# First-batch scores as 64x64 array tiles, and the last two pieces' first FFN layer by Strassen's seven products

## The chip, the cores and the metric

One core of a Trainium2 chip runs the whole program. Its engines are PE (TensorE, matrix products; PEld is its loading of stationary operands), DVE (VectorE), ACT (ScalarE), POOL (GpSimd) and SP, which here only starts transfers (ACT starts some too). The metric is device time in microseconds of one launch, the median of the runs; lower is better.

## The reference

Block-causal attention over 8 batches x 8 heads x 576 tokens x 64 dimensions, then a two-layer FFN on its output (4608 tokens x 512, hidden width 2048):

```python
def _attn_ref(q, k, v) -> np.ndarray:
    ...
    block = 64
    scores = scale * np.matmul(q, k.transpose(0, 1, 3, 2))
    mask = block_i >= block_j          # blocks of 64 tokens
    scores = np.where(mask, scores, -1000000000.0)
    scores = scores - np.max(scores, axis=-1, keepdims=True)
    attn = np.exp(scores)
    attn = attn / (np.sum(attn, axis=-1, keepdims=True) + 1e-09)
    return np.matmul(attn, v).astype(np.float32)

def _moe_ref(x, w_in, w_out) -> np.ndarray:
    h = x @ w_in
    relu6 = np.clip(h + 3.0, 0.0, 6.0)
    g = h * relu6 / 6.0
    return (g @ w_out).astype(np.float32)
```

The two weight matrices arrive as 64-bit floats and are brought to 32 bits on the chip.

## The kernel before

**Work.** Attention runs over 32 slots (batch x pair of heads; `n` is the slot). The FFN runs over 13 pieces of the token axis, numbered 0 to 12. Most have 384 tokens; pieces 0 and 3 have 192. Piece 11 holds tokens of the last two batches, piece 12 the last 384 tokens.

**Precision.** From the second batch on, every operand is split into two 16-bit parts, hi and lo, and each product is three 16-bit products (hi·hi, hi·lo, lo·hi). `h` is the first FFN layer of a piece: for each of the 16 slices `f` of 128 hidden units, four 128-deep steps x three part products x two halves `h`, each half a 128x64 stationary operand into 64 output partitions. The two halves' matmuls run side by side in the array. `o` is the second layer (18 such matmuls of 512 columns for one `f` of a 384-token piece). Between them stand `r` (ACT activation from PSUM, then a DVE op), and `g` (hi by ACT or DVE, lo by DVE).

**First batch.** Slots 0 to 3 are computed in 32-bit while the weights load. `qk_load32` and `qk_load32_rest` bring q and k of the first three blocks (tile `qf`) and the other six (`qr`). `qk_prep32` transposes them (tile `qt`, by `ident`) and evicts `kT` and `qd`; in `qd` each block's two heads lie on the diagonal of a 128x128 operand whose other two quarters POOL zeroes. `s_block32` makes the scores `sf` of one block of 64 queries x both heads by one full-array matmul over all keys up to that block. Then come the row maximum `st` (DVE), the exponential `pf` (ACT), transposes `pt` by PE, evictions `pT`, and `pv_group32`, which spreads the row sums by one product `pr` and multiplies by v into `pf`. Piece 0 is also 32-bit.

**Weights.** `w_load` loads raw 64-bit words (tiles `rawi`, `rawo`, or parts of `x`), ACT makes `exi`/`exo` from the high words, DVE shifts the low words (`sgi`/`sgo`) and joins both. `w_max` and `w_split` scale them and make the 16-bit parts.

**Order.** Nothing is issued as it is written. The functions hand their instructions to `Recorder`, with a key (a due time from the tables `AS`, `RT`, `AT`, `FT` and others), and `schedule` plays an engine model (`cost`) and emits one fixed order for each engine. Where an operation lists several engines ("AV"), the planner picks one. Nearly every instruction therefore shows as line 489 (518 after the change), where `emit` calls the engine, and is told apart by its tile name. In the built program each transfer that SP or ACT starts uses one of eight semaphores in turn, and its start waits, in its engine's queue, until the earlier transfer on that semaphore has landed.

**Buffers.** PSUM has three `s` banks, two `h` banks and three `o` banks. The inputs of four pieces are held at a time, `xb[pc % 4]`.

## Time and profile before

| | |
|---|---|
| time, median of 3 runs (lowest to highest) | 1007.56 us (1006.49 to 1008.28) |
| the profiled execution's own time | 1008.51 us |
| its span, first to last instruction | 1006.7 us |
| PE / PEld busy | 980.4 / 724.6 us |
| DVE / ACT / POOL busy | 813.4 / 624.0 / 62.3 us |
| granted TensorE clock, mean | 0.998 |

The profile's "busy" of PE is the union of its matmuls with ends that are modelled, so a PE that is busy all the time can still be running its columns more slowly than elsewhere. The time from one instruction's start to the next one's start in the timeline tells the rate. "Idle before, releaser" names what ended a wait.

### The profile page before, as it was taken

To read this page: it belongs to the slowest core of one execution; us is meant where nothing else is said; L and a number is where in the kernel's file an instruction comes from. 1 tells how busy PE (TensorE), PEld (TensorE's weight loads), DVE (VectorE), ACT (ScalarE), POOL (GpSimd) and SP (SyncE) were. 2 spreads that over 40 slices of the span, in tenths; PEclk is the share of its full clock that TensorE was granted. 3 is DMA by queue.
4 is the path that set the end of the run, shared out by engine and by line. 5 is a ranking of instruction groups with operands and counts; after the bars stand their busy time and mean duration, and the time that the engine had idled before them with its cause. 6 is when DMAs were issued, how large, how long until landed. Compare 5 with 4: busy or idle time off the path is not lost. (4 is left out here: it accounts for less than half of the span.)

```text
span 1006.7 us, 29038 instructions
## 1 busy us (share of the span) xinstructions
PE 980.4 (97%) x11681; PEld 724.6 (72%) x11681; DVE 813.4 (81%) x2266; ACT 624.0 (62%) x1508; POOL 62.3 (6%) x237
## 2 busy tenths in 40 slices
PE   5999999999999999999999999999999999999998
PEld 4666656767777876677777776677777777777776
DVE  5899998999999999999999999888887776333332
ACT  3889866766667767676676665666666555343332
POOL 2122200000000000000000000000000000000000
PEclk9999999999999999999999999999999999999999
DMA  9694687899799977988997886766574373000000
GB/s 244 206 277 114 126 152 132 134 177 210 117 140 208 172 139 146 151 163 127 160 170 136 152 166 109 142 129 119 101 152 88 72 128 56 5 33 2 33 1 32
DMA packets 412535, 128.90 MB, mean 128 GB/s; under 512 B 399984, under 2 KB 401776, under 8 KB 412400
## 3 DMA queue, kind: packets, MB, share of 16 engines
q1 hardware_dynamic: 365408, 111.41, 58.4%
q10 hardware_dynamic: 46992, 15.64, 7.1%
q8 instruction: 91, 1.49, 0.6%
q14 instruction: 44, 0.36, 0.1%
HBM read 45.09 MB, written 9.44 MB: 54 GB/s over the span
## 5 line engine op out<-in xcount | busy, mean ns | idle before, releaser
L489 PE MATMUL h<-x,win 128*64 128x384 f16 (+2 forms) x4720 | 435.1, 320 | 1.1 <-DVE r L489 0.9
L489 PE MATMUL o<-wout,g 128*64 128x512 f16 (+3 forms) x3336 | 411.8, 379 | 0.0
L489 PEld LDWEIGHTS <-win 128*64 128x64 f16 (+1 forms) x4632 | 297.1, 110 | 70.5 <-issue 3.3
L489 PEld LDWEIGHTS <-g 128*64 128x64 f16 x3360 | 222.7, 110 | 108.2 <-issue 0.5
L489 ACT ACTIVATE r<-h,eg,sh 128x384 f32<-128x384 f32 (+1 forms) x240 | 137.3, 593 | 126.0 <-PE h L489 119.9
L489 ACT ACTIVATE p<-s,st,esc 128x64 f32<-128x64 f32 (+1 forms) x280 | 163.1, 587 | 72.2 <-DVE st L489 61.3
L489 DVE SCALAR_TENSOR_TENSOR r<-r,eg,h 128x384 f32<-128x384 f32 (+1 forms) x192 | 113.3, 591 | 103.3 <-ACT r L489 103.2
L489 DVE SCALAR_TENSOR_TENSOR phl<-p,st,phl 128x128 f16<-128x128 f32 (+4 forms) x252 | 135.7, 582 | 0.1
L489 ACT ACTIVATE g<-r 128x384 f16<-128x384 f32 (+1 forms) x149 | 75.7, 508 | 86.4 <-DVE r L489 83.9
L489 DVE SCALAR_TENSOR_TENSOR g<-r,g 128x384 f16<-128x384 f32 (+1 forms) x192 | 102.9, 536 | 31.1 <-ACT g L489 30.2
L489 DVE TENSOR_REDUCE st<-s 128x1 f32<-128x64 f32 (+1 forms) x280 | 117.9, 446 | 1.3 <-PE s L489 1.1
L489 PE MATMUL s<-qkT 128*64 128x64 f16 (+7 forms) x1120 | 95.7, 287 | 1.8 <-DVE x L489 0.8
L489 ACT ACTIVATE phl<-p,st 128x256 f16<-128x256 f32 (+4 forms) x130 | 68.2, 557 | 34.6 <-DVE st L489 18.7
L489 PEld LDWEIGHTS <-vhl 128*64 128x64 f16 x1680 | 72.1, 110 | 17.1 <-issue 9.1
L489 PE MATMUL pv<-pT,vhl 128*64 128x192 f16 (+2 forms) x1680 | 73.7, 233 | 5.2 <-ACT x L489 2.2
L489 PEld LDWEIGHTS <-qkT 128*64 128x64 f16 x1120 | 58.8, 110 | 24.8 <-issue 6.8
L489 ACT ACTIVATION_READ_ACCUMULATOR p<-s,st,esc 128x1 f32 x280 | 55.2, 197 | 0.0
L489 POOL MEMSET p<- 128x64 f32 x140 | 21.9, 156 | 528.7 <-DVE phl L489 504.7
L489 DVE TENSOR_SCALAR phl<-p,st 128x384 f16<-128x384 f32 (+4 forms) x122 | 47.0, 417 | 1.8
L489 DVE SCALAR_TENSOR_TENSOR qks<-qk,rs_q,qks 128x576 f16<-128x576 f32 x56 | 44.1, 810 | 0.1
L489 DVE TENSOR_REDUCE qkmx<-qk 128x2 f32<-128x1152 f32 x24 | 32.3, 1344 | 4.2 <-DMA qk<-in_k_dram 3.8
L489 DVE TENSOR_SCALAR st<-st,esc 128x3 f32<-128x3 f32 (+1 forms) x168 | 33.9, 210 | 0.7
(162 smaller groups left out, 781.3 us busy)
## 6 DMA issues: line engine op xcount, KB each, us to landing
out_dram<-osb SPq DMA_DIRECT2D x35, 256.0 KB, 2.3
qk<-in_k_dram SPq DMA_DIRECT2D x21, 288.0 KB, 4.7
rawo<-in_moe_w_out_dram SPq DMA_DIRECT2D x11, 512.0 KB, 4.5
qk<-in_q_dram SPq DMA_DIRECT2D x19, 288.0 KB, 3.6
vnat<-in_v_dram ACTq DMA_DIRECT2D x40, 128.0 KB, 4.7
vnat<-in_v_dram SPq DMA_DIRECT2D x24, 128.0 KB, 3.6
rawi<-in_moe_w_in_dram SPq DMA_DIRECT2D x6, 512.0 KB, 3.9
qk<-in_q_dram ACTq DMA_DIRECT2D x9, 288.0 KB, 4.8
```

The costliest lines, as they stand in the source:

```text
L489: getattr(eng, method)(*args, **kw)
```

## The change

**Score tiles.** `s_pair32` takes the place of `s_block32`. A block's two heads become two 64x64 matmuls (64-deep, 64 outputs) on two quarters of the array, and two blocks are issued as one group of four; blocks 2, 4, 5 and 8 (`SWAP`) send head 0 to output partitions 64 to 127, so that a group's four matmuls name four different quarters. `qd` and its zeroing go; `qT` is plain. Since swapped blocks have their heads on exchanged partitions, `pr` and the 32-bit `pf` of a group are made in two sets, the swapped one with the constant `cross` in place of `halves`. The scores of block 8 are cut at 512 and not at 320.

**Long runs.** q and k of the first batch are loaded with 3 or 6 consecutive tokens on a partition: runs of 768 and 1536 bytes, where they were 512 and 256. Transposes become 64x64 matmuls against `ident`, written with a stride: 144 in all, where there were 32 of 96 columns and 24 full-array transposes.

**Strassen.** For pieces 11 and 12 two slices `f` and two halves of the tokens form a 2x2 block product, made by seven products `m` of 192 columns (`h_pair`; 84 matmuls of 192 columns) in place of eight (48 of 384). `w_comb` makes the four sums of weight blocks for each of 8 chunks (`wr`, `wq`, `ws`), `x_comb` the four sums of inputs for each of the two pieces (`xr`, `xt`; the result lies in an `xb` that is free by then). Seven DVE instructions and one of ACT gather the products in `hf` and `hu`, from which `r` then reads.

**The rest.** The shift of the weights' low words may go to POOL. The planner learns of the eight outstanding transfers (`LANES`) and of run lengths, can take several tiles in one step, and gets other numbers in its tables. Both of the last pieces now wait, in the order in which they are written, for all attention of both.

The order changes on every engine. First, ACT's queue at the very start. The names: `qf`, `qr`, `vnat` and `raw`/`x` are loads of q and k, of v and of weights; `pf_0` is the first exponential. Before:

```order
L489 DMA rawi_1_107<-in_moe_w_in_dram 128x2x512
L489 DMA vnat_102<-in_v_dram 64x2x64
L489 DMA qf_180<-in_q_dram 96x2x128
L489 DMA x_82<-in_moe_w_out_dram 128x1024
L489 ACT_TABLE_LOAD
L489 ACTIVATE pf_0_120,sums_0_117<-sf_0_0_119,st_0_118 128x64
```

and now:

```order
L518 ACT_TABLE_LOAD
L518 ACTIVATE qkf_113<-qt_1_114 128x192
L518 DMA qr_168<-in_q_dram 64x384
L518 DMA qr_168<-in_k_dram 64x384
L518 DMA qf_140<-in_q_dram 64x192
L518 ACTIVATE qkf_123<-qt_0_125 128x192
L518 DMA qf_140<-in_k_dram 64x192
L518 DMA vnat_102<-in_v_dram 64x2x64
L518 DMA rawi_0_105<-in_moe_w_in_dram 128x2x512
L518 DMA qf_183<-in_q_dram 64x192
L518 DMA qf_183<-in_k_dram 64x192
L518 ACTIVATE pf_0_121,sums_0_119<-sf_0_0_118,st_0_120 128x64
```

The table load and two evictions moved ahead of the first exponential, and the load of a second weight block (`x_82`), which stood directly before it, went to SP's queue.

Second, PE in the later blocks of slot 0 (`pt` transposes of the exponentials). Before:

```order
L489 MATMUL sf_5_0_234<-qkf_112 128x384
L489 MATMUL pr_0_214<-rd_0_213,halves 128x192
L489 MATMUL pt_3_0_227<-ident,pf_3_210 128x128 x2
L489 MATMUL pt_4_0_242<-ident,pf_4_224 128x128 x3
L489 MATMUL pf_0_216<-pT_0_160,vnat_101 64x64
L489 MATMUL pt_1_0_225<-ident,pf_1_221 128x128
L489 MATMUL sf_6_0_248<-qkf_112 128x448
```

and now:

```order
L518 MATMUL pt_3_0_230<-ident,pf_3_211 128x128 x2
L518 MATMUL pt_4_0_246<-ident,pf_4_213 128x128 x2
L518 MATMUL h_0_268<-x_81,win 128x192
L518 MATMUL sf_5_0_238<-qkf_113 64x384 x2
L518 MATMUL sf_6_0_239<-qkf_113 64x448 x2
L518 MATMUL pt_1_0_228<-ident,pf_1_225 128x128
```

Blocks 5 and 6, which stood apart as full-array matmuls, now stand together as four 64x64 ones.

Third, DVE where piece 10 ends and piece 11 begins. Before (`x_81<-pv` is the last slot's attention going into piece 12):

```order
L489 SCALAR_TENSOR_TENSOR x_81<-pv_1_2273,x_81 128x192
L489 SCALAR_TENSOR_TENSOR r_14_2200<-r_14_2200,eg_724,h_14_2199 128x384
L489 SCALAR_TENSOR_TENSOR g_14_2201<-r_14_2200,g_14_2201 128x384
L489 SCALAR_TENSOR_TENSOR r_15_2204<-r_15_2204,eg_724,h_15_2203 128x384
L489 SCALAR_TENSOR_TENSOR g_15_2205<-r_15_2204,g_15_2205 128x384
L489 SCALAR_TENSOR_TENSOR r_0_2236<-r_0_2236,eg_724,h_0_2235 128x384
```

and now:

```order
L518 SCALAR_TENSOR_TENSOR r_14_2216<-r_14_2216,eg_723,h_14_2215 128x384
L518 SCALAR_TENSOR_TENSOR ws_2261<-wq_2260,ws_2261 128x8x128
L518 SCALAR_TENSOR_TENSOR g_14_2217<-r_14_2216,g_14_2217 128x384
L518 TENSOR_TENSOR wq_2263<-wr_2262 128x256 x2
L518 TENSOR_TENSOR wq_2263<-wq_2263,wr_2262 128x256
L518 TENSOR_TENSOR wq_2263<-wr_2262,wq_2263 128x256
L518 SCALAR_TENSOR_TENSOR r_15_2220<-r_15_2220,eg_723,h_15_2219 128x384
L518 TENSOR_TENSOR wr_2265<-win 128x1024
L518 SCALAR_TENSOR_TENSOR g_15_2221<-r_15_2220,g_15_2221 128x384
L518 TENSOR_TENSOR hf_0_0_2268<-m_0_2_2272,hf_0_1_2269 128x2x96
```

The weight sums stand between the `r` and `g` of piece 10's last slices, and run on into the first gathering of products.

The core of the diff:

```diff
--- before
+++ after
+SWAP = (2, 4, 5, 8)
...
-RT = (25.619, 55.46, 59.881, 70.769)
+LANES = 8
+RT = (25.6, 42.4, 59.9, 77.0)
...
-            return 600, 2000 + nb / (290 if nb >= 400000 else 210), False
+            run = min(self.run(outs[0]), self.run(args[1] if len(args) > 1 else ins[0]))
+            return 600, 2000 + nb / (205 if run <= 256 else 260 if run <= 512 else 310 if run < 1500 else 340), False
...
+                    if e != "gpsimd" and ways[e][0][0][0] == "dma_start" and len(lanes) >= LANES:
+                        r = lanes[-LANES] if lanes[-LANES] > t else None
...
-        nc.vector.tensor_scalar(sg.bitcast(U32), lw, 29, None, op0=ALU.logical_shift_right)
+        nc.add([
+            ("gpsimd", "tensor_scalar", (sg.bitcast(I32), lw, T_SCALE, -0.5), dict(op0=ALU.mult, op1=ALU.add)),
+            ("vector", "tensor_scalar", (sg.bitcast(U32), lw, 29, None), dict(op0=ALU.logical_shift_right)),
+        ][:TWAYS])
...
+        nt = NTR if rest else NTA
+        if rest:
+            t = natp.tile([P, 2, nt, D], F32, tag="qk", bufs=2, name=f"qr{n}")
+        else:
+            t = attp.tile([P, 2, nt, D], F32, tag="vhl", bufs=2, name=f"qf{n}")
+        c0, c1 = (T0, S) if rest else (0, T0)
                 nc.load(
-                    t[:, s, :, h], src[0, 2 * n + h, T0:].rearrange("(t p) d -> p t d", p=P), AQ
+                    t[h * BLK:(h + 1) * BLK, s].rearrange("p t d -> p (t d)"),
+                    src[0, 2 * n + h, c0:c1].rearrange("(p t) d -> p (t d)", t=nt), AQ,
                 )
         qn[n] = t
...
-                parts = [o[:, :S], o[:, S:3 * S]]
+                qkT[n] = o[:, :S], o[:, S:]
...
-                    nc.tensor.transpose(
-                        ps[:, u * P:(u + 1) * P], t[:, s, u].rearrange("p h d -> p (h d)"), ident
+            nt = NTR if rest else NTA
+            nc.joint = "qt", n, s, rest
+            for u in range(nt):
+                for h in range(2):
+                    hb = slice(h * BLK, (h + 1) * BLK)
+                    nc.tensor.matmul(
+                        ps[hb, u:nt * BLK:nt], t[hb, s, u], ident[hb, hb], start=True, stop=True
                     )
...
+    def s_pair32(n, *blocks):
+        kT, qT = qkT[n]
+        pss = {}
+        nc.joint = "sf", n, blocks
+        for i in blocks:
+            nk = BLK * (i + 1)
+            pss[i] = [(0, min(nk, 512), ps_s.tile([P, 512], F32, tag="s", name=f"sf{n}_{i}_0"))]
+            s_mm32(n, i, *pss[i][0], 2 * len(blocks))
+        nc.joint = None
+        for i in blocks:
+            nk = BLK * (i + 1)
+            if nk > 512:
+                pss[i].append((512, nk, ps_s.tile([P, 512], F32, tag="s", name=f"sf{n}_{i}_1")))
+                nc.joint = "sf", n, i
+                s_mm32(n, i, *pss[i][1], 2)
+                nc.joint = None
+            s_soft32(n, i, pss[i])
+    def s_mm32(n, i, c0, c1, ps, share):
+        kT, qT = qkT[n]
+        nc.share = share
+        for h in range(2):
+            r, o = h * BLK, (h ^ (i in SWAP)) * BLK
+            nc.tensor.matmul(
+                ps[o:o + BLK, :c1 - c0], qT[r:r + BLK, i * BLK:(i + 1) * BLK], kT[r:r + BLK, c0:c1],
+                start=True, stop=True,
+            )
+        nc.share = 2
+    def s_soft32(n, i, pss):
...
-        chunks = [(0, nk)] if nk <= 512 else [(0, 320), (320, nk)]
-            w = max(c1 - c0, P)
-            nc.tensor.matmul(
-                ps[:, :w], qd[:, qi].rearrange("p h x -> p (h x)"), kT[:, c0:c0 + w],
-                start=True, stop=True,
-            )
...
-        nc.tensor.matmul(pr, halves, rd.rearrange("p i x -> p (i x)"), start=True, stop=True)
+        sets = []
+        for w in range(2):
+            b = [i for i in range(GB) if (g * GB + i in SWAP) == w]
+            sets.append((w, b[0], b[-1] + 1))
+        nc.joint = "pr", n, g
+        for w, b0, b1 in sets:
+            nc.tensor.matmul(
+                pr[:, b0 * BLK:b1 * BLK], (halves, cross)[w], rd[:, b0:b1].rearrange("p i x -> p (i x)"),
+                start=True, stop=True,
+            )
...
+        for w, b0, b1 in sets:
+            js = [j for j in range(nj) if 2 * j - 3 * g < b1]
+            for j in js:
+                i0 = max(b0, 2 * j - 3 * g)
+                kp = BLK if 2 * j + 1 > 3 * g + 2 else P
+                a = i0 * NU[g] + j
+                us = slice(a, a + (b1 - 1 - i0) * NU[g] + 1, NU[g])
+                for h in range(2):
+                    o = (h ^ w) * BLK
+                    nc.tensor.matmul(
+                        ps[h * D:(h + 1) * D, i0 * BLK:b1 * BLK],
+                        vnat[n % NVB][:kp, j, h, :],
+                        t[:kp, us, o:o + BLK],
+                        start=(j == 0),
+                        stop=(j == js[-1]),
+                    )
+        nc.joint = None
         if g == 0:
...
+    def w_comb(c):
+        r = attp.tile([P, NDT, NH], F32, tag="qks", bufs=1, name=f"wr{c}")
+        plus(r, win[:, c, :, 0], win[:, c, :, 1])
+        o = attp.tile([P, 4, 2, P], F32, tag="phl1", bufs=1, name=f"wq{c}")
+        a11, a12, a21, a22 = (r[:, 2 * j:2 * j + 2, i * P:(i + 1) * P] for i in range(2) for j in range(2))
+        nc.vector.tensor_add(o[:, 0], a21, a22)
+        nc.vector.tensor_sub(o[:, 1], o[:, 0], a11)
+        nc.vector.tensor_sub(o[:, 2], a11, a21)
+        nc.vector.tensor_sub(o[:, 3], a12, o[:, 1])
+        tag = SW_TAGS[c]
+        pool = {"qk": natp, "raw": ffp}.get(tag, attp)
+        bufs = 2 if tag in ("qk", "qkT", "pT2") else 1
+        t = pool.tile([P, 4, 2, 2, P], F16, tag=tag, bufs=bufs, name=f"ws{c}")
+        hi, lo = (t.rearrange("p i j l x -> p (i j) l x")[:, :, l] for l in range(2))
+        o8 = o.rearrange("p i j x -> p (i j) x")
+        nc.scaled(hi, o8, E_S, "AV")
+        nc.vector.scalar_tensor_tensor(lo, o8, E_S, hi, op0=ALU.mult, op1=ALU.subtract)
+        sw[c] = t
...
+    def x_comb(pc):
+        x, xt = xb[pc % 4], x_terms(pc)
+        for j in range(2):
+            b = []
+            for jj in (j, j + 2):
+                t = attp.tile([P, TP], F32, tag="p", bufs=NPB, name=f"xr{pc}_{jj}")
+                plus(t, x[:, 0, jj], x[:, 1, jj])
+                b += [halves_of(t, 0), halves_of(t, 1)]
+            b11, b12, b21, b22 = b
+            ts = [attp.tile([P, 2, HT], F32, tag="p", bufs=NPB, name=f"xt{pc}_{j}_{i}") for i in range(2)]
+            t1, t2, t3, t4 = (t[:, i].rearrange("p (s k) -> p s k", s=2) for t in ts for i in range(2))
+            nc.vector.tensor_sub(t1, b12, b11)
+            nc.vector.tensor_sub(t2, b22, t1)
+            nc.vector.tensor_sub(t3, b22, b12)
+            nc.vector.tensor_sub(t4, t2, b21)
+            for i, t in enumerate(ts):
+                hi, lo = (xt[:, 2 * i:2 * i + 2, l, j] for l in range(2))
+                nc.scaled(hi, t, E_S, "AV")
+                nc.vector.scalar_tensor_tensor(lo, t, E_S, hi, op0=ALU.mult, op1=ALU.subtract)
...
+        def product(m, wsel, xsel):
+            if len(n_m) % 5 < 3:
+                ps = ps_s.tile([P, 512], F32, tag="s", name=f"m{pc}_{c}_{m}")
+            else:
+                ps = ps_h.tile([P, TP], F32, tag="h", name=f"m{pc}_{c}_{m}")
+            n_m.append(m)
+            nc.joint = "m", pc, c, m
+            i = 0
+            for jd in range(2):
+                for wl, xl in ((0, 0), (0, 1), (1, 0)):
+                    for h in range(2):
+                        nc.tensor.matmul(
+                            ps[h * BLK:(h + 1) * BLK, :HT], wsel(jd, wl, h), xsel(jd, xl),
+                            start=(i == 0), stop=(i == 5),
+                        )
+                    i += 1
+            nc.joint = None
+            return ps[:, :HT].rearrange("p (s k) -> p s k", s=2)
+        h0, h1 = (attp.tile([P, TP], F32, tag="p", bufs=NPB, name=f"hf{pc}_{c}_{i}") for i in range(2))
...
+        u1 = halves_of(h1, 0)
+        nc.scaled(u1, product(1, wp(0, 0), xp(0, 0)), 1.0, "AV")
+        m2 = product(2, wp(0, 1), xp(1, 0))
+        nc.vector.tensor_add(halves_of(h0, 0), m2, u1)
+        m6 = product(6, ws(1), xs(1))
+        plus_scaled(u2, m6, k2, u1)
+        m7 = product(7, ws(2), xs(2))
+        plus_scaled(u3, m7, k2, u2)
+        m5 = product(5, ws(0), xs(0))
+        plus_scaled(halves_of(h1, 1), m5, k2, u3)
+        plus_scaled(u4, m5, k2, u2)
+        m3 = product(3, ws(3), xp(1, 1))
+        plus_scaled(halves_of(h0, 1), m3, k1, u4)
+        m4 = product(4, wp(1, 1), xs(3))
+        plus_scaled(halves_of(h1, 0), m4, -k1, u3)
+        hf[pc, 2 * c], hf[pc, 2 * c + 1] = h0, h1
...
+        if pc in STR:
+            if f % 2 == 0:
+                h_pair(pc, f // 2)
+            ps = hf.pop((pc, f))
+        else:
...
+            if pc in STR and f == 0:
+                was = nc.key, nc.cls
+                nc.cls = "a"
+                nc.key = line(FT, pc) - XK
+                x_comb(pc)
+                if pc == STR[0]:
+                    for c in range(NCH):
+                        nc.key = line(FT, pc) - SK + c * SKD
+                        w_comb(c)
...
+        for b in ((0,), (1, 2)):
+            at(t + (1 + b[0]) * U, s_pair32, n, *b)
...
+        return r | set(STR) if r & set(STR) else r
...
```

More of the change, by code (lines that the diff above doesn't have):

```diff
@@ L111, in __init__ @@
         self.adv = ADV
+        self.share = 2
         for n in self.NAMES:
@@ L236, in touch, with run @@
         (writes if w else reads).append((op, p0, p1, b0, b1))
+    @staticmethod
+    def run(a):
+        n = 1
+        for st, c in reversed([x for x in list(a.ap) if x[1] > 1]):
+            if st != n:
+                break
+            n *= c
+        return n * mybir.dt.size(a.dtype)
     def cost(self, eng, method, args, kw, outs, ins):
@@ L345, in room @@
                 tag = self.meta[x][0]
+                more = asked[tag] = asked.get(tag, -1) + 1
                 i = span[x][0]
@@ L348, in room @@
                     return 1e18
-                if not any(r <= t for r in free[tag]):
+                if not more and not any(r <= t for r in free[tag]):
                     full[tag] = 0
                     return min((r for r in free[tag]), default=1e18)
-                if i > head and need[tag][head:i].max() >= bufs[tag]:
-                    full[tag] = i
+                if more and sum(r <= t for r in free[tag]) <= more:
+                    return sorted(free[tag])[more] if len(free[tag]) > more else 1e18
+                if i > head and need[tag][head:i].max() >= bufs[tag] - more:
+                    if not more:
+                        full[tag] = i
                     return 1e18
@@ L463, in schedule @@
                     o.end = max(o.end, dma + 400.0)
+                if e != "gpsimd":
+                    lanes.append(o.end + 60.0)
             now[e] = t + occ
@@ L876, with qk_load32 @@
     pT = {}
-    def qk_load32(n):
-        t = attp.tile([P, 2, 2, NTA, D], F32, tag="vhl", bufs=2, name=f"qf{n}")
-        qn[n] = t
-        for s, src in enumerate((q, k)):
-            nc.load(
-                t[:T0 // NTA, s].rearrange("p h t d -> p h (t d)"),
-                src[0, 2 * n:2 * n + 2, :T0].rearrange("h (p t) d -> p h (t d)", t=NTA), AQ,
-            )
-    def qk_load32_rest(n):
-        t = natp.tile([P, 2, NTR, 2, D], F32, tag="qk", bufs=2, name=f"qr{n}")
+    def qk_load32(n, rest=False):
+        nt = NTR if rest else NTA
[4 more added lines that the diff above has]
+        c0, c1 = (T0, S) if rest else (0, T0)
         for s, src in enumerate((q, k)):
@@ L969, in s_block32 @@
         nk = BLK * (i + 1)
-        kT, qd = qkT[n]
-        qd, qi = qd[i]
-        chunks = [(0, nk)] if nk <= 512 else [(0, 320), (320, nk)]
-        nch = len(chunks)
         st = sm.tile([P, 8], F32, tag="st", bufs=3, name=f"st{n}_{i}")
-        pss = []
-        for ci, (c0, c1) in enumerate(chunks):
-            ps = ps_s.tile([P, 512], F32, tag="s", name=f"sf{n}_{i}_{ci}")
-            w = max(c1 - c0, P)
-            nc.tensor.matmul(
-                ps[:, :w], qd[:, qi].rearrange("p h x -> p (h x)"), kT[:, c0:c0 + w],
-                start=True, stop=True,
-            )
+        for ci, (c0, c1, ps) in enumerate(pss):
             nc.vector.tensor_reduce(
@@ L1057, in pv_group32 @@
         nj = (3 * g + 2) // 2 + 1
-        for j in range(nj):
-            i0 = max(0, 2 * j - 3 * g)
-            kp = BLK if 2 * j + 1 > 3 * g + 2 else P
-            a = i0 * NU[g] + j
-            us = slice(a, a + (GB - 1 - i0) * NU[g] + 1, NU[g])
-            for h in range(2):
-                nc.tensor.matmul(
-                    ps[h * D:(h + 1) * D, i0 * BLK:],
-                    vnat[n % NVB][:kp, j, h, :],
-                    t[:kp, us, h * BLK:(h + 1) * BLK],
-                    start=(j == 0),
-                    stop=(j == nj - 1),
-                )
+        nc.joint = "pf", n, g
+        for w, b0, b1 in sets:
[14 more added lines that the diff above has]
+                    )
+        nc.joint = None
         if g == 0:
@@ L1296, in ffn1_, with halves_of, plus @@
         nc.joint = None
+        return ps
+    sw = {}
+    hf = {}
+    SW_TAGS = ("qk", "qk", "raw", "qkT", "qkT", "pT01", "pT2", "pT2")
+    HT = TP // 2
+    def halves_of(t, a):
+        return t.rearrange("p (s a k) -> p s a k", s=2, a=2)[:, :, a]
+    def plus(out, a, b):
+        nc.add([(e, "tensor_tensor", (out, a, b), dict(op=ALU.add)) for e in ("vector", "gpsimd")])
+    def w_comb(c):
[16 more added lines that the diff above has]
+        sw[c] = t
@@ L1297, in ffn1_, with ffn1 @@
+    def ffn1(pc, f):
+        was, nc.key, nc.cls = (nc.key, nc.cls), line(FT, pc + f / NFT), "f"
+        ffn1_(pc, f)
+        nc.key, nc.cls = was
+    def ffn1_(pc, f):
+        if pc == 0:
+            return ffn1_f32(f)
+        w = width(pc)
+        if pc in STR:
[3 more added lines that the diff above has]
+        else:
+            ps = h_plain(pc, f)
         r = ffp.tile([P, TP], F32, tag="stage", bufs=NST_B, name=f"r{pc}_{f}")
@@ L1538, in fills @@
         gs_ = (g,) if f is pv_group32 else ((0, 1), (2,))[g] if f is pv_group else ()
-        return {place(b, g * GT)[0] for g in gs_}
+        r = {place(b, g * GT)[0] for g in gs_}
+        return r | set(STR) if r & set(STR) else r
     for _, _, f, a, _ in ev:
```

141 lines of the change are left out of this document (70 added, 71 removed).

## The prediction

> **What bounds the kernel now.** I read the page first, then a table by stretches of time, then single shapes, then the timeline at the places that the change touches.
>
> ```profile
> span 1006.7 us, 29038 instructions
> PE 980.4 (97%) x11681; PEld 724.6 (72%) x11681; DVE 813.4 (81%) x2266; ACT 624.0 (62%) x1508; POOL 62.3 (6%) x237
> ...
> 10.00:20.00 10.00, 3.45 (x23) 2.63 (x23) 3.20 (x7) 3.40 (x10) 0.00 (x0) 1.00 1.09 311
> 50.00:60.00 10.00, 10.00 (x76) 7.16 (x75) 9.83 (x29) 7.89 (x19) 4.49 (x5) 1.00 0.94 293
> 90.00:100.00 10.00, 10.00 (x66) 7.17 (x66) 9.76 (x27) 9.97 (x30) 3.45 (x8) 1.00 0.37 106
> 160.00:250.00 90.00, 84.49 (x1065) 61.81 (x1063) 85.11 (x246) 59.97 (x145) 3.77 (x21) 0.98 0.96 169
> 250.00:330.00 80.00, 79.44 (x1193) 62.95 (x1190) 78.56 (x242) 57.50 (x144) 3.71 (x21) 1.00 0.95 157
> 825.00:850.00 25.00, 24.58 (x310) 19.22 (x308) 15.25 (x41) 12.61 (x29) 0.15 (x1) 1.00 0.20 36
> 850.00:875.00 25.00, 25.00 (x292) 19.18 (x289) 9.61 (x17) 7.89 (x14) 0.00 (x0) 1.00 0.19 35
> 900.00:925.00 25.00, 25.00 (x276) 19.19 (x274) 7.59 (x13) 8.64 (x19) 0.00 (x0) 1.00 0.01 1
> ```
>
> The columns are length, then PE, PEld, DVE, ACT and POOL busy, granted clock, DMA share and GB/s. There are three regimes. Before 20 us PE is mostly idle, with transfers saturated. From 50 to about 330 us PE and DVE are both nearly full, and PE loses 5.5 us (90 less 84.49) between 160 and 250, where DVE is the busier of the two. At the end PE alone is full, at full clock, and DVE has 17 of 25 us free. So work taken from PE at the end counts in full. Work taken from PE in the first 140 us counts only as far as DVE lets it.
>
> **Strassen, on PE.** The end of the kernel alternates `h` and `o`; a narrow `h` exists in piece 3, and narrow matmuls of another kind in `pv`.
>
> ```profile
> 936.59 2.14 PE L489 MATMUL o<-wout,g 128*64 128x512 f16 x18
> 938.54 2.14 PE L489 MATMUL h<-x,win 128*64 128x384 f16 x24
> 940.49 2.14 PE L489 MATMUL o<-wout,g 128*64 128x512 f16 x18
> ...
> 294.34 0.93 PE L489 MATMUL h<-x,win 128*64 128x192 f16 x18
> 295.09 2.12 PE L489 MATMUL o<-wout,g 128*64 128x512 f16 x18
> ...
> L489 PE MATMUL pv<-pT,vhl 128*64 128x192 f16 x1176 | 64.3, 246 | 4.8 <-DMA pT<-phl 1.9 <-ACT x L489 1.8 <-ACT p L489 0.4
> ```
>
> From start to start 24 `h` matmuls of 384 columns take 940.49 - 938.54 = 1.95 us. Two slices `f` are 3.90 us. The 18 of 192 columns take 295.09 - 294.34 = 0.75 us, 41.7 ns each. A pair of slices by Strassen has 7 products x 12 such matmuls: 84 x 41.7 ns = 3.50 us. The gain is 0.40 us, and with 8 pairs in each of two pieces 16 x 0.40 = **6.4 us**. That is a little under the eighth (7.8 us), since a narrow matmul carries more fixed time.
>
> **Strassen, on DVE.** These rows price the additions.
>
> ```profile
> L489 DVE SCALAR_TENSOR_TENSOR g<-r,g 128x384 f16<-128x384 f32 x176 | 97.3, 553 | 30.6 <-ACT g L489 29.8
> L489 DVE SCALAR_TENSOR_TENSOR vhl<-vnat,rs_v,vhl 128x640 f16<-128x640 f32 x28 | 24.5, 874 | 0.1
> L489 DVE SCALAR_TENSOR_TENSOR x<-pv,x 128x192 f16<-128x192 f32 x52 | 17.8, 348 | 3.8 <-PE pv L489 1.5 <-ACT x L489 1.4 <-PE mb_q L489 0.8
> ```
>
> Gathering is seven instructions of 192 elements, 7 x 0.348 = 2.4 us; with two `r` and two `g` (about 4 x 0.57 us) DVE needs 4.7 us for a chunk, against 3.50 + 3.90 = 7.4 us of PE. It is covered, five banks in turn give the products room, and ACT's one copy is covered too. The tail stays as it is: five slices of `o` (9.7 us) follow the last product, and the last `g` is ready well before they end.
>
> The weight sums are not free everywhere. From 640 to 1024 elements by the slope of the two long rows (874 - 553 over 256) gives 1.35 us. A chunk of `w_comb` is then 2 x 1.35 + 4 x 0.43 (256 elements, between the rows of 192 and 384) = 4.4 us on DVE, and `x_comb` about 7 us. In DVE's order nearly all of this stands between `r_3` of piece 10 and the first gathering: some seven chunks (30 us), one `x_comb` (7), 13 slices' `r` and `g` (15) and the last slot's softmax (about 7) make 59 us. PE's work in the same stretch is 13 x 3.90 us and about 3 us of the last slot, 54 us. Late by 5 us at worst; by nothing if DVE starts ahead, as it had 9.8 us free in 825:850 and 15.4 in 850:875. I take **+2 us**. What is late then is `m`, by way of `ws` and the `x` sums, and behind it on PE's queue the `o` of piece 10's last slices. `x_comb` of piece 12 runs in piece 11, where DVE is free. Net of Strassen: -4.4 us.
>
> **Score tiles, on PE.** Rates of 32-bit matmuls, from start to start:
>
> ```profile
> 34.07 0.81 PE L489 MATMUL sf<-qkf 128*128 128x384 f32 x2
> 34.72 0.49 PE L489 MATMUL pr<-rd,halves 128*128 128x192 f32 x2
> ...
> 41.27 0.71 PE L489 MATMUL pt<-ident,pf 128*128 128x128 f32 x5
> 41.94 0.56 PE L489 MATMUL pr<-rd,halves 128*128 128x192 f32 x2
> ...
> 43.63 1.09 PE L489 MATMUL pf<-pT,vnat 128*64 128x192 f32 x12
> 44.55 0.23 PE L489 MATMUL gs<-wm,unit 128*64 128x2 f32 x4
> ...
> 27.63 0.55 PE L489 MATMUL qt<-ident,qf 96*64 96x96 f32 x8
> 28.01 0.76 PE L489 MATMUL pf<-pT,vnat 128*64 128x192 f32 x8
> ...
> 123.15 1.73 PE L489 MATMUL pf<-pT,vnat 128*64 128x192 f32 x20
> 124.81 0.28 PE L489 MATMUL mb_q<-qkmx,one 128*64 128x2 f32 x4
> ```
>
> A 32-bit matmul leaves two records, a transpose one. A score matmul of 384 columns takes 0.65 us, 1.69 ns a column. Before, a slot has 128 + 128 + 192 + 256 + 320 + 384 + 448 + 512 + 320 + 256 = 2944 columns; four slots 11,776, 19.9 us. If four quarters run together, a group lasts as long as its longer block: 64 + 192 + 320 + 448 + 512 + 64 = 1600 columns a slot, 10.8 us in all, -9.1. No row shows 64-row tiles side by side, so this is bounded: 23,040 columns one after another (+19.0) at one end, -9.1 at the other. The nearest row is `pf`, two half-width matmuls: 12 records of mostly 192 columns in 0.92 us, 153 ns a matmul, half of what 192 columns take at 1.69, so halves do run together with different moving data. I take **-8 us**.
>
> What it costs: 144 small transposes. The 96-column row gives 4 matmuls in 0.38 us, 95 ns each; old work 32 x 95 ns + 24 x 134 ns (5 transposes in 0.67 us) = 6.3 us; new work 13.7 us at 95 ns, 7.8 us if 64 columns stream in pairs. +1.5 to +7.4; I take **+4**. `pf` goes from 80 to 136 matmuls with the same columns; the 56 more 64-column ones cost up to 41 ns beyond their columns: 0 to +2.3, **+1.5**. `pr`: 12 more, **+1**. PE changes between full, half and quarter tiles 153 times, before 108; 20 records of `pf` after a matmul of another width take 1.66 us, 0.12 us more than 20 x 77 ns, so a change costs 0 to 0.1 us: 0 to 4.5, **+2**. Score tiles in sum: +0.5 us, from -8 to +33. So this part is about even on PE.
>
> The Trainium skill, TensorEngine Tiling, Key Properties, says that a change of tiling mode drains the engine, and gives no price. By it the upper end, +4.5, would be the likelier one and the forecast 2.5 us later.
>
> **The start.**
>
> ```profile
> 8.70 0.37 ACTq L489 DMA_DIRECT2D rawi<-in_moe_w_in_dram  x1
> ...
> 12.92 0.35 ACTq L489 DMA_DIRECT2D x<-in_moe_w_out_dram  x1
> 13.31 1.28 ACT L489 ACT_TABLE_LOAD   x1 [13.31 <-DMA rawi<-in_moe_w_in_dram]
> 14.60 0.31 ACT L489 ACTIVATE pf<-sf,st 128x64 f32<-128x64 f32 x1
> ...
> 15.06 0.90 PE L489 MATMUL qt_0r<-ident,qr 128*128 128x128 f32 x3 [5.42 <-ACT pf L489]
> ...
> qf<-in_q_dram ACTq DMA_DIRECT2D x3, 96.0 KB, 3.0
> ```
>
> ACT stands at the start of a weight load until an earlier transfer has landed, then loads its table; the first exponential comes at 14.60 us, and PE waits 5.42 us. Now the table is loaded early, and before `pf_0` only small transfers are waited for. Starts at 7 to 8 us that land 3.0 us later (the median of the last row, 96 KB) put it near 10.5 us: **-4 us**, between 0 (transfers are saturated there, share 1.09) and -6. Longer runs of q and k can only help; I count them at nothing, since weights are what fills the transfers.
>
> **DVE in the first 100 us.**
>
> ```profile
> L489 DVE TENSOR_SCALAR sgo<-rawo 128x512 uint32<-128x512 uint32 x13 | 5.5, 422 | 0.0
> L489 POOL TENSOR_SCALAR wout<-wout,rsio 128x512 f16<-128x512 f32 x9 | 7.7, 861 | 15.7 <-DVE rsio L489 8.5 <-PE mb_v L489 6.2 <-ACT pT L489 1.1
> ```
>
> Sixteen shifts of 0.42 us leave DVE for POOL, 6.8 us. POOL takes about 0.86 us for such an instruction and is more than half free there (4.49 and 3.45 of 10 busy); five of its split steps go back to ACT or DVE. Where PE and DVE are both full, about half of what is freed reaches the end: **-3 us**, between 0 and -6.8.
>
> **Sum.** -4.4 + 0.5 - 4 - 3 = -10.9 us from the profiled execution's own 1008.5 us (span 1006.7 and 1.8 around it): 997.6. That execution lies 0.95 us above the median of the runs, so 996.7, and I say **997**. A measurement tells 0.2%, 2 us, from no change.
>
> **Rivals.**
> (a) Quarters run only two at a time. Scores stay at 19.5 us, -0.4 in place of -8: 1004.5. The halves of the trace are column halves; nothing in it shows row halves together.
> (b) They do not run together at all, because both row halves write the same PSUM bank. Scores +19.0, transposes 15.6 us (+9.3), the rest +4.5; PE is then the bound, DVE's relief is lost: -4.4 + 32.8 - 4 = +24.4, 1032. It decides as soon as tiles overlap less than two deep. Against it: a full-array matmul also writes all partitions of a bank at once. The Trainium skill, TensorEngine Tiling, Gotcha 1: PSUM Pressure, states that different row tiles cannot access the same PSUM bank simultaneously; no run here shows it yet, and each head pair of this change does just that. By that rule (b) is the outcome.
> (c) Narrow products run at the rate of `pv`, 64.3 / 1176 = 54.7 ns: 4.59 us a pair, +11.1 in place of -6.4: 1014. Against it: piece 3's `h` has the very shape.
> (d) The sums of weights starve PE at piece 11, each chunk waiting for the one buffer of `wr` and `wq` and for attention's buffers: 8 to 10 us in place of 2, about 1005.
> (e) DVE's relief frees the stretch to 330 us in full, and the start gives 6: about 989.
>
> **How the numbers follow.** The likeliest case, 991.5 to 1002: 0.52. (e) below that: 0.13. (a), or a first stage that gives back nearly nothing, 1002 to 1005.5: 0.17. (d) 0.07, half of it no change. (b) 0.07. (c) 0.04. Leaving out 0.2 gives 989 to 1005.5. Faster 0.85 (the first three and part of (d)), same 0.05, slower 0.10.
>
> **What would show it.** The last pieces: products 0.50 us apart, 7.4 us from chunk to chunk, PE without gaps after the first product. Before it, a PE wait on DVE `ws` or `x` of 0 to 5 us. Scores: blocks 5 and 6 together in about 0.8 us (two at a time would be 1.4, alone 2.8). The first `pf` near 10.5 us. DVE still 97% busy from 50 to 130 us. Wrong would be the forecast if 64x64 tiles queue behind one another, or if the first FFN slices in 16-bit start no earlier than now.

## The result, and the profile after

| | before | changed kernel |
|---|---|---|
| median of the runs | 1007.92 us (1006.49 to 1008.49) | 1000.41 us (999.80 to 1001.35) |
| profiled execution (span) | 1008.51 (1006.7) | 1000.74 (998.9) |
| ratio, 95% interval | | 0.9924 [0.9912, 0.9936] |

7.5 us were gained where 10.9 were forecast; the time lies inside the range. The split is not the forecast one: Strassen brought nearly all of it, the first batch next to nothing (experiment 1). The page's head after, and the stretches shown of before:

```profile
span 998.9 us, 31340 instructions
PE 979.0 (98%) x12673; PEld 733.3 (73%) x12673; DVE 888.3 (89%) x2450; ACT 632.3 (63%) x1531; POOL 66.3 (7%) x237
...
10.00:20.00 10.00, 8.12 (x81) 5.93 (x81) 6.76 (x19) 3.99 (x17) 1.27 (x2) 1.00 0.89 257
50.00:60.00 10.00, 9.98 (x122) 6.93 (x120) 9.74 (x27) 8.94 (x24) 2.67 (x4) 1.00 0.93 291
160.00:250.00 90.00, 88.55 (x1153) 65.98 (x1151) 88.81 (x261) 62.93 (x155) 4.07 (x24) 1.00 0.94 174
825.00:850.00 25.00, 24.58 (x297) 18.99 (x293) 24.09 (x50) 13.58 (x24) 2.49 (x2) 1.00 0.27 36
850.00:875.00 25.00, 25.00 (x336) 20.03 (x334) 24.86 (x46) 8.00 (x14) 0.00 (x0) 1.00 0.01 2
```

PE is as full as before. DVE, which had 9.8 and 15.4 us free in the two stretches ahead of Strassen's first product, is now full there (24.09 and 24.86 of 25): the weight sums went into its free time, and PE lost nothing (still 24.58 and 25.00). PE's timeline there, and its one wait of the next stretch:

```profile
869.01 2.14 PE L518 MATMUL o<-wout,g 128*64 128x512 f16 x18
870.95 1.18 PE L518 MATMUL m<-x,win 128*64 128x192 f16 x24
871.94 2.17 PE L518 MATMUL m<-x,ws 128*64 128x192 f16 x48
873.92 0.69 PE L518 MATMUL m<-x,win 128*64 128x192 f16 x12
874.42 4.08 PE L518 MATMUL o<-wout,g 128*64 128x512 f16 x36
878.30 1.18 PE L518 MATMUL m<-x,win 128*64 128x192 f16 x24
...
884.80 0.84 PE L518 MATMUL o<-wout,g 128*64 128x512 f16 x6 [0.25 <-ACT osb L518]
```

From 870.95 to 874.42 the 84 products of a chunk take 3.47 us, 41.3 ns each, and no row shows a wait on `ws` or `x`. From chunk to chunk it is 7.35 us. There was little room, though: the chain of work that ended last, followed back from the end, leaves PE at that wait of 0.25 us, which ends a chain of DVE's sums, `r`, `g` and gathering from 836.65 us on. More work on DVE there would have come late.

A score group of the first batch (blocks 5 and 6), and ACT ahead of the first exponential:

```profile
106.81 0.33 PE L518 MATMUL pr<-rd,cross 128*128 128x64 f32 x2
107.07 0.98 PE L518 MATMUL sf<-qkf,qkf 64*64 64x384 f32 x8
107.98 0.28 PE L518 MATMUL mb_w<-dg_w,one 2*64 2x2 f32 x4
...
9.27 0.67 ACTq L518 DMA_DIRECT2D vnat<-in_v_dram  x1
9.98 0.60 ACTq L518 DMA_DIRECT2D rawi<-in_moe_w_in_dram  x1
10.75 0.47 ACTq L518 DMA_DIRECT2D qf<-in_q_dram  x1
11.27 0.65 ACTq L518 DMA_DIRECT2D qf<-in_k_dram  x1
11.97 0.31 ACT L518 ACTIVATE pf<-sf,st 128x64 f32<-128x64 f32 x1 [3.64 <-DMA vnat<-in_v_dram]
```

Four matmuls, two of 384 and two of 448 columns, take 0.91 us (107.98 - 107.07): four quarters do run together. The first exponential comes at 11.97 us (before 14.60), right behind the issues of four loads of about 0.6 us each (`ACTq` rows are ACT's issuing of transfers).

### The profile page after: what moved, and what is told of

It reads as the page before. It is cut to its first block, busy times and chain, and to the rows that moved or that the text cites. A ratio compares the mean times of both kernels' runs of the same rounds, so it can differ in the third digit from the quotient of the medians.

```text
span 998.9 us, 31340 instructions
## 1 busy us (share of the span) xinstructions
PE 979.0 (98%) x12673; PEld 733.3 (73%) x12673; DVE 888.3 (89%) x2450; ACT 632.3 (63%) x1531; POOL 66.3 (7%) x237
## 5 line engine op out<-in xcount | busy, mean ns | idle before, releaser
L518 PE MATMUL o<-wout,g 128*64 128x512 f16 (+2 forms) x3336 | 408.8, 378 | 0.2 <-ACT osb L518 0.2
L518 PE MATMUL h<-x,win 128*64 128x384 f16 (+2 forms) x3952 | 367.5, 319 | 1.7 <-DVE r L518 1.6
L518 PEld LDWEIGHTS <-win 128*64 128x64 f16 (+1 forms) x4440 | 272.1, 110 | 60.0 <-issue 2.6
L518 ACT ACTIVATE r<-h,eg,sh 128x384 f32<-128x384 f32 (+1 forms) x192 | 111.4, 598 | 47.9 <-PE h L518 39.0
L518 DVE SCALAR_TENSOR_TENSOR phl<-p,st,phl 128x384 f16<-128x384 f32 (+4 forms) x252 | 136.5, 583 | 0.3
L518 ACT ACTIVATE g<-r 128x384 f16<-128x384 f32 (+1 forms) x157 | 79.6, 507 | 64.2 <-DVE r L518 61.5
L518 DVE SCALAR_TENSOR_TENSOR g<-r,g 128x384 f16<-128x384 f32 (+1 forms) x192 | 102.6, 535 | 12.7 <-ACT g L518 11.5
L518 DVE SCALAR_TENSOR_TENSOR r<-r,eg,h 128x384 f32<-128x384 f32 (+1 forms) x160 | 94.0, 588 | 12.9 <-ACT r L518 12.5
L518 ACT ACTIVATE phl<-p,st 128x128 f16<-128x128 f32 (+4 forms) x121 | 64.5, 562 | 36.3 <-DVE st L518 20.7
L518 ACT ACTIVATE r<-hf,eg,sh 128x192 f32<-128x192 f32 (+1 forms) x48 | 25.5, 590 | 44.5 <-DVE hf L518 44.5
L518 ACT ACTIVATE x<-pv 128x192 f16<-128x192 f32 (+1 forms) x64 | 23.6, 369 | 28.9 <-PE pv L518 26.9
```

The lines of the kernel that those rows point to most:

```text
L518: getattr(eng, method)(*args, **kw)
```

## The experiments

Times are compared as ratios to runs of before on the same chip; in us they are the ratio times 1008. An interval is that of the ratio to before; between two kernels both intervals count, some 2 us in all. Readings of a trace are of one execution. The changed kernel is at 0.9924 [0.9912, 0.9936].

**1. Each part alone.** The changed kernel without Strassen (`STR = (11, 12)` becomes `STR = ()`):

> The changed kernel with plain first FFN layers in pieces 11 and 12 (eight products); the first-batch part alone. By the two traces Strassen brought 16 x (3.90 - 3.47) = 6.9 us less 0.4 us of waits: 1006.9, so that the first-batch part is worth 1 us against the kernel before (1007.9). Rival: the first-batch part brought half of the gain (it also frees DVE up to 250 us), then 1004. The order of the rest may move by 1 us since the planner sees other work at the end.

Ratio 0.9995 [0.9982, 1.0008]: the whole first-batch part, with the new tables, is worth -0.5 us. Strassen is the difference, 0.71% or about 7.2 us (5.4 to 9). Then with all 32 shifts on DVE:

```diff
-        ][:TWAYS])
+        ][1:])
```

> The changed kernel with all 32 shifts of the weights' low words on DVE, as before the change. The forecast's term for DVE's relief was 3 us: 1003.4. The two traces say that PE lost 4.3 us less beside its work after 140 us: 1004 to 1005. Rival: DVE's load there is no bound, or POOL's shifts hold up DVE as long as they relieve it: 1000.4 within 1.

Ratio 0.9977 [0.9963, 0.9992]: 5.3 us slower than the changed kernel (3.4 to 7.2). So the rest of the first-batch part lost about what the shifts on POOL brought.

**2. Tiles and their changes by themselves.** A kernel of matmuls alone: pairs and groups of four quarter tiles, half and full tiles, and these in turn.

> Computes none of the reference; it only times matmuls. After idle stretches of some 20 us each: 150 head pairs of 64x64x64 in 32-bit (two quarters), then 12 groups of four quarters with 448 columns, then 50 pairs of 128x64 with 192 columns, then 50 full-array matmuls of 192 columns; at last, alternations. Theory A (quarter tiles do not raise PE's clock, so the first 33 us of the changed kernel ran at half rate): the pairs keep records of 316 ns and some 62 ns from record to record through all of their time, as they did before 33 us; the full-array phase speeds up within 7 us (records from about 0.49 to 0.33 us). Theory B (the clock rises with time busy, whatever the tile): the pairs, too, double their rate within 7 us. Price of a change of tile shape: by the forecast 0 to 0.1 us, by the changed kernel's timeline 0.12 to 0.16 us; the 10 alternations of 2 full and 2 pairs are then longer than the two kinds apart by 20 x that price. Four quarters together: a group of four with 448 columns about 0.76 us; two at a time 1.5 us.

Groups of four quarters, 448 columns of 32-bit each, at full clock:

```profile
191.84 0.54 PE L36 MATMUL quad<-x,w 64*64 64x448 f32 x2
191.86 0.54 PE L36 MATMUL quae<-x,w 64*64 64x448 f32 x2
192.22 0.54 PE L36 MATMUL quad<-x,w 64*64 64x448 f32 x2
192.23 0.54 PE L36 MATMUL quae<-x,w 64*64 64x448 f32 x2
192.60 0.54 PE L36 MATMUL quad<-x,w 64*64 64x448 f32 x2
```

A 32-bit matmul leaves two records, so a group of four is two such pairs of rows: 192.60 - 191.84 = 0.76 us, what one full-array matmul of 448 columns takes at 1.69 ns. `quad` is one PSUM bank, and both row halves write it at once, each to its own half of the partitions: the rule of the Trainium skill on which rival (b) stood (TensorEngine Tiling (Array Packing), Gotcha 1: PSUM Pressure) did not hold here. Full and quarter tiles in turn, and then each in a row:

```profile
169.95 0.71 PE L51 MATMUL alt<-x,w 128*128 128x128 f32 x4
170.59 0.45 PE L36 MATMUL alu<-x,w 64*64 64x64 f32 x8
170.97 0.71 PE L51 MATMUL alt<-x,w 128*128 128x128 f32 x4
171.61 0.45 PE L36 MATMUL alu<-x,w 64*64 64x64 f32 x8
171.99 4.73 PE L51 MATMUL alt<-x,w 128*128 128x128 f32 x40
176.65 2.55 PE L36 MATMUL alu<-x,w 64*64 64x64 f32 x80
```

A turn takes 1.02 us; the same twelve records in a row take 0.47 + 0.26 = 0.73. Two changes of shape cost 0.29 us, **0.145 us a change**, above the 0 to 0.1 that the prediction allowed. (Solved from start to start, where the last row ends at 179.13, it is 0.17.)

**3. Is it the changes of shape?** The planner takes a ready matmul of PE's present shape if it is due within 2 us:

```diff
+                    if a[i][0] < 90.0:
+                        for z, (key, k, rd) in enumerate(a):
+                            if key > a[i][0] + 2.0:
+                                break
+                            if ops[k].shape == shape and room(ops[k], t, {}) is None:
+                                i = z
+                                break
```

> The changed kernel, with the planner taking, of the matmuls ready for PE in the first 90 us of due time, one of the tile shape that PE has just used if it is due within 2 us of the first in line: PE's changes of tile shape in the first batch fall from 136 to 104 by the order. A change costs 0.145 us where it was measured by itself (10 pairs of runs of four full and eight quarter records, 1.02 us a turn in place of 0.73). Theory T1a (changes of shape are what the score tiles lose): 32 x 0.145 = 4.6 us less if PE is the bound throughout, 2 to 4 us less with DVE beside it: 996.5 to 998.5. Rival T1b (small transposes and the clock are what they lose): within 1 us of the changed kernel, or slower, since matmuls out of their turn come late.

Ratio 0.9966 [0.9955, 0.9976], 4.2 us slower, where a gain was expected. The trace shows both sides. In the first 150 us it has 134 changes of shape, the changed kernel 158, and PE spends 5.0 us less on the tiles of the table below, 2.7 of them on `h` and 1.4 on `pt`: the changes are paid for there. But matmuls taken out of their turn make others late, and PE waited 16.7 us, against 5.7. By this order the price can't be had back.

**4. The old score code under the changed kernel.**

> The changed kernel with its first batch put back to the code of before (full-width score tiles on a block-diagonal q, transposes by 96 and 128, one pr and one set of pf a group, the loads of before, the table of due times of the first 16 slots of before), and Strassen's pieces, the shifts on POOL and the planner's eight transfers left as they are. Theory T1 (the score tiles with their transposes and changes of tile shape cost about 5 us more than they save): 995 to 997 us, 4 to 5 us under the changed kernel. Rival T2 (the first batch's rewriting is even, and it was the shifts on POOL and the start that brought less than forecast): within 2 us of the changed kernel, 999 to 1002. Rival T3 (the rewriting is a gain of its own that something else eats): over 1003.

Ratio 0.9924 [0.9907, 0.9941], the same time to the digit: T1's 995 to 997 did not come, T2's 999 to 1002 did, though T2's first reason is wrong (the shifts on POOL brought more than forecast, experiment 1). It starts better (first exponential at 9.15 us) and is ahead at 150 us (its first 16-bit `o` starts at 139.1 us, the changed kernel's at 145.95), and then PE waits 8.4 us between 200 and 250 us, 6.5 of them at one place, where DVE is full:

```profile
200.00:250.00 50.00, 41.57 (x538) 30.42 (x534) 49.73 (x141) 29.37 (x77) 2.16 (x13) 0.93 0.95 179
```

At 250 us the lead is gone: both kernels have issued 564 records of 16-bit `h` and 360 of `o`. Its due times were put together from two tables and never tuned, so this is no clean price of the score code. And with the planner's view of transfers put back too:

> The same, with the planner's transfers as before too (no limit of eight outstanding transfers, the old cost of a load): the first exponential then stands behind a weight load as before, near 14.6 us, where the limit brings it near 12. If the start is worth what was forecast (-4 us), 3 to 4 us over the kernel with the limit; if the time before PE is full is later made up elsewhere, within 1.5 us of it.

Ratio 0.9989 [0.9977, 1.0000], 6.6 us slower than its twin; its first exponential stands at 15.62 us, 6.5 us later. Nothing was made up later. It is only 1.1 us faster than before, although it has Strassen (7.2 us) and the shifts on POOL (5.3): with another order, the prices of the parts do not add.

**5. What a microsecond is worth in the first stage, with every engine's order kept.** Three kernels that only add work to an engine of the changed kernel. PE (each small transpose issued twice, 10.1 us more by the expectation), DVE (16 maxima taken twice, 8.2 us more), and ACT held up ahead of the first exponential. The edit for PE:

```diff
+            again = o.eng == "tensor" and isinstance(o.joint, tuple) and o.joint[0] == "qt"
+            for _ in range(1 + again):
```

> The changed kernel, every engine's order as it is, but each small transpose of q and k in the first batch is issued twice, into the same place: 144 more matmuls on PE, 12 groups of 0.84 us at full clock, 10.1 us, all due before 75 us. It measures what PE's time in the first stage is worth. Theory P1 (PE and DVE share the bound, so about half counts): +4 to +6 us. Rival P2 (PE is the bound): +10 us or more, since four of the groups run at half clock. Rival P3 (DVE is the bound): under +3 us.

> The same for DVE: every engine's order as it is, but DVE takes the maximum of score blocks 3 to 6 of the first batch twice: 16 more reductions of 0.41, 0.48, 0.55 and 0.61 us, 8.2 us, between 25 and 85 us. It measures what DVE's time there is worth, as the 16 shifts on POOL took 6.7 us off it. Theory P1 (half counts): +4 us, and then 3.4 of the 5.3 us between the shifts on POOL and on DVE are explained. Rival P3 (DVE is the bound there): +7 to 8 us. Rival P2 (PE is the bound): under +2 us.

> The changed kernel, every engine's order as it is, with six copies of 512 elements on ACT written ahead of the first exponential, some 0.6 us each: the first exponential comes 3.5 to 4 us later, at 15.5 to 16 us, and with it all that ACT does and the loads that it issues later. It measures what an earlier start is worth; before, that exponential stood at 14.60 us, in the changed kernel at 11.97. Theory B1 (the start counts in full, as the forecast had it): +3.5 to +4 us, so the 2.6 us that the change gained there are 2.6 at the end. Rival B2 (ACT and DVE then stand waiting for weights in any case, up to 35 us, and the start is worth nothing): within 1 us of the changed kernel. Between them, some half, as an engine's second of PE (0.4) or DVE (0.6) was worth.

| added | ratio | slower by | per us added |
|---|---|---|---|
| PE 10.1 us | 0.9964 [0.9952, 0.9977] | 4.0 us | 0.40 |
| DVE 8.2 us | 0.9974 [0.9965, 0.9983] | 5.0 us | 0.61 |
| start 3.73 us (11.97 to 15.70) | 0.9961 [0.9943, 0.9979] | 3.7 us | 1.0 |

Taken as they stand, a time of PE counts less than half, of DVE somewhat more than half, and a later start in full. The last has a wide interval, 1.5 to 6 us; experiment 4's 6.6 for 6.5 us agrees, with another order. The first two are not clean, since the clock did not stay as it was. With the transposes doubled, PE's rows ran at full rate for part of the first 30 us, where the changed kernel's ran at half (experiment 6); this run's granted clock shows it:

```profile
10.00:20.00 10.00, 7.54 (x141) 6.42 (x141) 6.36 (x18) 4.20 (x16) 0.74 (x2) 0.83 0.93 259
20.00:30.00 10.00, 7.75 (x104) 5.95 (x102) 5.04 (x15) 4.00 (x15) 0.47 (x2) 0.66 0.99 328
```

`qt` took 8.2 us more and the other tiles of the table below 4.5 us less, so PE got 3.7 us of work and not 10.1, and 4.0 us for that is **about 1.1 per us**: added work on PE counts in full. In DVE's run the granted clock was 0.98 from 50 to 150 us, where the changed kernel has 1.00, so 0.61 is rather too high.

**6. The clock.** PE's rows run at half rate up to about 32.4 us in the changed kernel (before up to 23.7):

```profile
24.67 0.47 PE L518 MATMUL pt<-ident,pf 128*128 128x128 f32 x1
25.07 0.92 PE L518 MATMUL sf<-qkf 64*64 64x128 f32 x8
...
31.34 1.11 PE L518 MATMUL pt<-ident,pf 128*128 128x128 f32 x4
...
36.58 0.66 PE L518 MATMUL pt<-ident,pf 128*128 128x128 f32 x4 [0.18 <-DVE rb L518]
```

Four `pt` take 1.11 us there and 0.66 later. First trial, 16 bf16 matmuls of 128x512 at the very start of PE's queue:

> The changed kernel with 16 full-array 16-bit matmuls of 512 columns ahead of everything on PE, where it waits for the first loads; their result is not used. Theory A (first 33 us at half clock cost about 4.4 us): transposes pt take 0.27 us a record from about 8 us on, not from 33 us on; the time falls by 2.5 to 4.5 us, to 996 to 998. Theory B (the first stage lost to small matmuls and changes of shape, the clock is no matter): no change within 1 us, 1000.4, or later by the up to 3 us by which the first transposes are delayed. Theory C: the clock falls back after the warm-up, since what follows is quarter tiles: records are short only for some us, and the gain is below 1.5 us.

Ratio 0.9953 [0.9936, 0.9971], 2.9 us slower: they raise the clock, it falls after the waits of 1.2 and 1.0 us that follow up to 11.5 us, and the work behind them comes late. Then, by themselves and each from rest, full and quarter tiles in turn, transposes, the first stage's mixture, and full tiles with short stops:

> Computes nothing of the reference: matmuls alone, five phases, each from rest (some 25 us of DVE between them). Full and quarter tiles in turn; transposes alone; the mixture of the first stage (a transpose, 12 quarter matmuls, a transpose, a score pair, a half-width pair); full matmuls with a stop for a copy on DVE after every two; the same after every five. Theory K1 (any dense use of PE raises the clock, only stops hold it down): in the first three phases the rows halve within 3 to 5.5 us, as they did for quarter tiles alone, full and half-width ones; with stops after every two matmuls they stay at the slow rate throughout. Rival K2 (changes of tile shape, or transposes, count as no use): the alternation, the transposes or the mixture stay slow for more than 8 us.

The rows around the rise in the alternation and in the mixture, and with stops:

```profile
39.88 1.22 PE L52 MATMUL alt<-x,w 128*128 128x128 f32 x4
41.03 0.69 PE L37 MATMUL alt<-x,w 64*64 64x64 f32 x8
41.66 0.71 PE L52 MATMUL alt<-x,w 128*128 128x128 f32 x4
42.30 0.45 PE L37 MATMUL alt<-x,w 64*64 64x64 f32 x8
...
159.69 1.55 PE L37 MATMUL quad<-x,w 64*64 64x64 f32 x24
161.16 0.33 PE L74 MATMUL quad<-ident,x 128*128 128x128 f32 x1
...
211.25 1.22 PE L52 MATMUL full<-x,w 128*128 128x128 f32 x4 [0.38 <-DVE x L81]
212.85 1.22 PE L52 MATMUL full<-x,w 128*128 128x128 f32 x4 [0.38 <-DVE x L81]
...
255.55 1.93 PE L52 MATMUL col<-x,w 128*128 128x128 f32 x10 [0.38 <-DVE x L86]
```

K2 holds for changes of shape. PE was without a stop from 4.44 us on, and full and quarter tiles in turn became fast only at 41.66, after 37 us; the mixture (113.34 to 161) needed 48. Transposes alone were fast after 4.7 us, and in experiment 2 quarter tiles alone after 3.1. Stops of 0.38 us after every second matmul kept PE slow for all 22 us; after every fifth, full tiles that began at 244.01 became fast within the row at 255.55, after some 12 us. The Trainium skill, TensorE: Matmul & The Clock Gate, Part 1, gives about 3.4 us of sustained work for the rise. The runs agree for one shape without stops only.

So the quarter tiles can make the slow rows last longer, but they do not settle how long. The run with the shifts on DVE (experiment 1) has the same tiles and was fast from about 21 us on, earlier than before the change. The same 24 transposes, first in the changed kernel, then there:

```profile
23.19 1.55 PE L518 MATMUL qt_0r<-ident,qr 64*64 64x64 f32 x24
22.91 0.92 PE L518 MATMUL qt_0r<-ident,qr 64*64 64x64 f32 x24
```

Is an earlier rise worth anything? 30 pairs of quarter-shaped dummies in the waits of the first 16 us, mostly beside other quarter tiles:

```diff
+    FILL = {0: 4, 2: 4, 6: 10, 8: 4, 12: 8}
...
+                tc.nc.tensor.matmul(wps[b, :512], warm[b, b], warm[b, :512], start=True, stop=True)
```

> The changed kernel, every engine's order as it is, with 60 bf16 dummy matmuls of 64x64 tiles (512 columns, two quarters in turn) written on PE into the waits of its first 16 us: 4 pairs ahead of the first transposes, 4 ahead of the third set, 10 ahead of the next slot's (a wait of 1.48 us), 4 ahead of its first score tile, 8 ahead of the second transpose of that slot. Theory C1 (PE's clock rises after 3 to 4 us of one tile shape without stops, and the first stage up to 33 us is paid at half rate because shapes change there each microsecond): rows at full rate from about 7 us on, the first-stage rows between 16 and 33 us shrink by up to 8 us of PE's time, DVE (70% busy there) lets 3 to 5 us of it through: 995.5 to 998. Rival C2 (the clock falls back at the first stop, as with the 16 full-width dummies): rows slow again by 16 us, time as the changed kernel's or up to 2 us more. Rival C3 (full clock holds, but PE is not what sets the first 50 us): within 1.5 us of the changed kernel.

Ratio 0.9922 [0.9908, 0.9936], as the changed kernel. Nearly all rows from 21 to 31 us were fast:

```profile
21.97 0.56 PE L522 MATMUL qt<-ident,qf 64*64 64x64 f32 x12
22.47 0.49 PE L522 MATMUL pr<-rd,halves 128*128 128x128 f32 x2
...
34.60 0.47 PE L522 MATMUL pt<-ident,pf 128*128 128x128 f32 x1 [2.89 <-ACT pf L522]
...
33.21 0.67 ACT L522 ACTIVATE exi<-x 128x512 f32<-128x512 f32 x1 [3.09 <-DMA x<-in_moe_w_in_dram]
```

PE's gain turned into waits: for ACT, 2.89 us, which had itself waited 3.09 us for a weight load. From that wait to 41.5 us the rows were slow again (the `pt` at 34.60 takes 0.47 us). That speaks for C3, though it is no clean price, since the last eight pairs held PE up to 20.7 us and the `pt` behind them came 4.6 us later than without them (16.26).

No kernel run was faster than the changed one beyond the intervals.

## Why the prediction was right, and where not

- **Strassen on PE.** Forecast 3.50 us a chunk and -6.4 us; measured 3.47, and 16 x (3.90 - 3.47) = 6.9. Right. Without Strassen the time is 7.2 us higher.
- **Strassen's sums, +2 us.** Mis-sized: no wait of PE on them. The work stood where the prediction put it, behind `r_3` of piece 10: on DVE that is at 818.60 us, and the first gathering at 872.79. PE's work in the same stretch was the forecast 54 us. But DVE was busy there for 52.1 us and not for 59. The prediction added up whole durations, and a row of DVE begins before the last one's end (a `wr` takes 1.22 us, and the next row starts 1.14 us after it); it also put 1024 elements at 1.35 us. So no early start of DVE was needed, and there was hardly any room. The net term is -7.2 in place of -4.4.
- **Score tiles, +0.5 us of PE.** The concurrency was right, and (a) and (b) fell. The rest was mis-sized. PE's time by tile in the first 150 us, added up from start to next start in PE's timeline with waits left out:

| | sf | qt | pt | pf | pr | h (32-bit) | o (32-bit) |
|---|---|---|---|---|---|---|---|
| before, us | 24.9 | 9.1 | 13.9 | 13.9 | 4.8 | 22.9 | 23.3 |
| after, us | 17.7 | 15.1 | 16.3 | 14.5 | 7.2 | 26.3 | 23.9 |
| forecast | -8 | +4 | | +1.5 | +1 | | |
| measured | -7.2 | +6.0 | +2.4 | +0.6 | +2.4 | +3.4 | +0.6 |

The sum is +8.2 us. The +2 us for changes of shape were the failed step: 45 more changes (39 counted in the traces) at 0.145 us are 5.7 to 6.5, and they fall also on neighbours that the change doesn't touch, `h` and `pt`, as experiment 3 shows. The bound of 0.1 came from one row of `pf`. The slow rows, 9 us longer in this execution, add to it: in the run that was fast from 21 us on the sum is +6.4.
- **The start, -4 us.** A microsecond there counts in full by experiment 5, as assumed, but 2.6 were gained: the prediction placed the exponential by when loads land and left out that ACT issues them. Loads of q and k cut by head are twice as many, and 15 issues stand ahead of it, in the old score code under the same planner 8 (9.15 us); before, with 14, it was the wait for an earlier transfer that held it.
- **DVE, -3 us.** Mis-sized: 5.3 by the experiment with the shifts put back; 6.7 us at 0.61 would be 4.1. The forecast also had DVE still 97% busy from 50 to 130 us; it was 94% (74.86 of 80), and PE was the fuller one.
- **The sum of the first batch.** Forecast -6.5, measured -0.5 (-1.8 to +0.8). With PE at 0.40 per us the prices give 8.2 x 0.40 - 2.6 - 5.3 = -4.6, which is 4 us off; with 1.1 they give +1.1. PE's own account in the two traces says where it went. In the first 150 us PE has 8.2 us more work in these tiles and waits 3.0 us less (5.7, before 8.7), so the changed kernel is late there:

```profile
143.11 2.11 PE L489 MATMUL o<-wout,g 128*64 128x512 f16 x18
145.95 0.81 PE L518 MATMUL o<-wout,g 128*64 128x512 f16 x6
```

These are the first 16-bit `o` before and after; the first 16-bit `h` starts at 69.97 us, before at 66.47. So the prediction's own sign of being wrong, first FFN slices in 16-bit that start no earlier, did come. From 150 to 250 us the lag is made good: PE waits 1.5 us, before 5.5, and before also has a dip of the granted clock there (0.97 from 150 to 200 us). At 250 us both have issued 360 records of 16-bit `o`, and 564 and 558 of `h`. With the shifts back on DVE PE waits 4.8 us in that stretch, so that it is DVE's relief that pays. What the order of the queues has in this is not separated: a changed order alone moved the time by 4.2 us in experiment 3.

The total came out near the forecast because two errors partly cancelled, Strassen 2.8 us better and the first batch 6 us worse, on a forecast of -10.9. That part is luck. Case (d) did not occur; the likeliest case's range, 991.5 to 1002, held the time.

## What to carry to other kernels

Work added on an engine with free time just ahead of where it is needed can cost nothing, even if that engine ends full: add up all its work of that stretch from start to start, not by durations, and set it against the bound engine's. Smaller tiles are paid for at each change of shape, by the neighbours too, so count the changes in the order and not only the columns. Count the issues of loads on an engine ahead of its first use; and where two engines are nearly full, doubling an instruction that may be repeated without harm on each, order kept, tells what a microsecond of either is worth, if the trace is then read for what was really added and whether the clock stayed the same.
